# A newly dealt order for a fused linear-attention and feed-forward kernel: all steps from the 60th on, the gates of its loads, and seven small steps on GpSimd

## The chip, the cores and the metric

The kernel runs on one core of a Trainium2 chip. The core has TensorE (PE, matrix products), VectorE (DVE), ScalarE (ACT), GpSimd (POOL) and SyncE (SP), and 16 DMA engines. Each engine works through a list of its own, in order, and waits at semaphores for the others. Results of TensorE land in PSUM, eight banks of 128 partitions x 512 fp32 numbers; everything else lies in SBUF. The metric is the device time of one execution in microseconds: the median of three runs before the change is 351.93 us (350.92 to 352.03).

## The reference

Inputs are q, k and v of 8 batches x 8 heads x 576 positions x 64 features, a feature matrix `w_phi` (64 x 128) and two feed-forward matrices (512 x 2048 and 2048 x 512).

```python
def phi(x):
    proj = np.einsum('bhsd,df->bhsf', x, w_phi)
    proj = proj - np.max(np.abs(proj), axis=-1, keepdims=True)
    return np.concatenate([np.exp(proj), np.exp(-proj)], axis=-1)
q_p, k_p = (phi(q), phi(k))
kv = np.einsum('bhsf,bhsd->bhfd', k_p, v)
z = np.sum(k_p, axis=2)
num = np.einsum('bhsf,bhfd->bhsd', q_p, kv)
den = np.einsum('bhsf,bhf->bhs', q_p, z)[..., None] + 1e-06
```

The attention output num / den, brought to 4608 tokens x 512, is the x of the feed-forward: `h = np.maximum(x @ w_in, 0.0)`, and the result is `(h * h) @ w_out`, 4608 x 512 in fp32.

## The kernel before

**Tiles.** The eight batches are treated one after the other. A batch has 576 tokens: 512 make a feed-forward chunk of their own (chunks 0 to 7), and the remaining 64 of all batches are collected in `xS` and make chunk 8. PE multiplies in bf16, blocks of 128 x 128 against up to 512 columns.

**Attention of a batch.** k and q are needed with their features on the partitions. In batches 0 and 1 PE transposes them itself (`pe_transposes`), and a copy on VectorE or ScalarE moves the block out of PSUM. From batch 2 on one DMA transpose each, issued on SP (`transposed`, L339), makes `kT` and `qT` out of the loaded `xk` and `xq`. `project` multiplies with `w_phi` (L355); the row maximum is taken on VectorE (k: L410, q: L517) and the two exponentials on ScalarE (k: L416, q: L592). The maximum itself goes into v: `em_ops` makes factors of it on ScalarE, `v_ops` multiplies v with them (L443). `kv_ops` sums k features times v on PE (L473, L478) and copies the sum to SBUF (the "kv copy", L196 on VectorE, L198 on ScalarE). `out_ops` multiplies q's features with it (L607), scales by the factor `en` (ScalarE L551, VectorE L619), divides (L627, L631) and turns the result into `xT`: in batch 0 on PE with a copy (L656), later by a DMA transpose on SP (L665).

**Feed-forward of a chunk.** `ffn_in` (L751; for chunk 0 `ffn_in_small`, L762, in pieces of 128 tokens) makes 512 columns of h in a PSUM bank. `relu_sq` takes the relu on ScalarE (L726) or VectorE (L728) into one of four buffers `hr`, and squares it into `h2` (L735). `ffn_out` (L816) sums four times four products to one 128 x 512 output tile, which is copied out of PSUM and stored from SP (L835). For the last tokens stands `last_out` (L780). The feed-forward of chunk c - 1 and c runs on PE beside the attention of later batches, so that PE always has something to do.

**Loads.** All loads of k, q, v, w_in and w_out are issued on GpSimd; they cast fp32 to bf16 on the way. From batch 2 on k, q and v of a batch come in four pieces of two heads each and two short ones for the last 64 tokens. Batches of the same parity share their buffers `xk`, `xq`, `xv`.

**What sets the order.** The program first lists all steps (1731 of them, numbered as they are listed; a step is the group of instructions that one `add` gives). `Plan.arrange` then emits them in the order of the table `ORDER`, with these tables beside it, all written out as numbers:

- `STATES` has a digit for each step that was given to `plan.either`: 1 puts it on the second engine named there. Relus, output copies, kv copies and the copies of transposed blocks can be on ScalarE or VectorE; v products and squares of the first batches or chunks can be on VectorE or GpSimd.
- `BASES` has the PSUM bank of each step that opens one.
- `GATES` names, for loads from batch 2 on, a step that must have ended before the load is issued. As GpSimd works in order, a load also waits for the gates of those ahead of it.
- `FILL` puts warm-up matmuls on PE ahead of a step (L885): the step's number, then bank, count, column.

So the position in `ORDER` counts only against steps of the same engine, and between engines only the data, the buffers and the gates hold a step back.

Of the kernel before, what the change touches and what calls it, by code (L numbers as in the profile page):

```python
# [111 lines left out]
def kernel(  # L112
# [15 lines left out]
    P = 128  # L128
# [47 lines left out]
    LENT = 2  # L176
# [9 lines left out]
    h2 = [ring(f"h2{c}_", 4, [4, TCH]) for c in range(2)]  # L186
# [130 lines left out]
    def attention(b):  # L317
        s2 = b % 2
        pe_in = b < 2
        first = b == 0  # L320
# [125 lines left out]
        def v_ops(g0, g1):  # L446

            gs = [4] if g0 == 4 else list(range(g0, g1))
            for sg in range(2):
# [13 lines left out]
                if b < LENT:  # L463
                    plan.either((o, "POOL", pool_cost(512 * (g1 - g0))))
# [256 lines left out]
    def relu_sq(c, g, dst, toks):  # L721
# [15 lines left out]
        if c < LENT:  # L737
            plan.either((o, "POOL", pool_cost(512)))
# [17 lines left out]
    def ffn_in_small(c, tt, mg):  # L756

        g = Bank(1, "hp")
        def fn():
            for i in range(4):  # L760
                for kc in range(KC):
                    pin(nc.tensor.matmul(out=ps1(g)[:, i * P : (i + 1) * P], lhsT=win[mg][:, kc, i * P : (i + 1) * P],  # L762
                                         rhs=xT[c % NXT][kc // 2][:, tt, kc % 2, :],
                                         start=(kc == 0), stop=(kc == KC - 1)))
        add("PE", pe_cost(16, 0.0565), fn, r=[("win", mg)] + x_toks(c, [tt]),
            w=[g], opens=g, what="f1")
        relu_sq(c, g, h2[c % 2][mg][:, :, tt * P : (tt + 1) * P], [("h2", c % 2, mg * 4 + i, tt) for i in range(4)])
# [266 lines left out]
```

## Time and profile before

| | before |
|---|---|
| median of three runs | 351.93 us |
| profiled execution | 352.42 us |
| its span, first to last instruction | 350.3 us |
| TensorE busy | 337.3 us |
| VectorE busy | 271.6 us |
| ScalarE busy | 228.7 us |
| GpSimd busy | 96.8 us |
| data moved by DMA | 46.69 MB |

The span is that of one execution taken by the profiler; the device time is longer by what lies around it. Matmuls are pipelined, so a busy PE says that one was in flight. In lines of the profile "x<-y" is a step's output and input by the program's names, "xN" a count, and "<- A" behind an idle time tells what ended it. PEld is PE's loading of weights; SPq, ACTq and POOLq are the queues of engines that issue DMAs.

### The profile page before, as it was taken

The numbers are of one execution on the slowest core, as the hardware profiler recorded it, in microseconds if no ns is written. First come the engines' busy times: TensorE is split into PE (matmuls) and PEld (weight loads), VectorE is DVE, ScalarE is ACT, GpSimd is POOL, SyncE is SP. The second block draws the span as 40 slices with busy tenths as digits, with TensorE's granted clock in tenths as the row PEclk, the third lists the DMA queues.
The fourth block names the chain that finished last, engine by engine and source line by source line (L and its number), as shares of the span: only waits on it lengthen the run. The fifth ranks groups of instructions, "written<-read, shape, count | busy, mean of one in ns | idle before, by whom it ended". The sixth has DMA issues, their size and how long they took to land.

```text
span 350.3 us, 8403 instructions
## 1 busy us (share of the span) xinstructions
PE 337.3 (96%) x3335; PEld 191.7 (55%) x3370; DVE 271.6 (78%) x520; ACT 228.7 (65%) x432; POOL 96.8 (28%) x144
## 2 busy tenths in 40 slices
PE   8889999999999999999999989999999999999994
PEld 5669976544654555465546544465455544444451
DVE  4999998899979988898889988789697923745030
ACT  4999897599779775987999684784766111233111
POOL 8735450397518600283100460010000000000000
PEclk9999999999999999999999999999999999999998
DMA  8999989799999997899999999778954521001016
GB/s 100 183 201 202 196 98 144 154 127 156 192 184 134 155 148 150 189 153 117 136 190 164 141 155 165 169 116 144 207 110 77 117 87 67 32 0 60 2 37 173
DMA packets 124327, 46.69 MB, mean 133 GB/s; under 512 B 92800, under 2 KB 119808, under 8 KB 124288
## 3 DMA queue, kind: packets, MB, share of 16 engines
q0 software_dynamic: 45216, 18.36, 46.9%
q1 hardware_dynamic: 78752, 27.50, 39.7%
q8 instruction: 26, 0.43, 0.5%
q10 hardware_dynamic: 320, 0.30, 0.4%
q14 instruction: 13, 0.11, 0.1%
HBM read 36.77 MB, written 9.44 MB: 132 GB/s over the span
## 4 chain that ended last, share of the span: by engine, by line
PE 84%; ACT 5%; DVE 4%; DMA 3%; issue 2%; DVEq 0%; ACTq 0%; POOLq 0%
PE psum L816 32%; PE psum L751 30%; PE psum L607 5%; PE psum L355 5%; PE psum L473 4%; PE psum L762 3%; DMA xT<-xo 2%; DVE va L443 2%; ACT qf L592 2%; PE psum L577 2%; PE psum L780 1%; DMA xk<-in_k_dram 1%; PE psum L478 1%; ACT kp L398 1%; DVE mq L517 1%
## 5 line engine op out<-in xcount | busy, mean ns | idle before, releaser
L816 PE MATMUL psum<-wout,h 128*128 128x512 bf16 x525 | 129.4, 379 | 2.6 <-issue 1.1
L751 PE MATMUL psum<-xT,win 128*128 128x512 bf16 x448 | 107.6, 379 | 1.2 <-DMA xT<-xo 1.2
L726 ACT ACTIVATE hr<-psum 128x512 bf16<-128x512 f32 x99 | 57.1, 596 | 63.4 <-PE psum L751 48.0
L816 PEld LDWEIGHTS <-h 128*128 128x128 bf16 x560 | 51.3, 98 | 55.9 <-issue 0.8
L751 PEld LDWEIGHTS <-win 128*128 128x128 bf16 x512 | 46.9, 98 | 53.6 <-issue 1.9
L735 DVE TENSOR_TENSOR h<-hr 128x512 bf16<-128x512 bf16 x143 | 56.3, 417 | 14.8 <-ACT hr L726 14.2
L592 ACT ACTIVATE qf<-psum 128x1024 bf16<-128x1024 f32 (+1 forms) x50 | 45.8, 945 | 7.6 <-PE psum L577 7.3
L517 DVE TENSOR_REDUCE mq<-psum 128x8 f32<-128x1024 f32 (+1 forms) x40 | 44.1, 1108 | 2.3 <-PE psum L355 1.1
L728 DVE TENSOR_SCALAR hr<-psum 128x512 bf16<-128x512 f32 x45 | 30.5, 686 | 18.8 <-PE psum L751 17.9
L410 DVE TENSOR_REDUCE mk<-psum 128x8 f32<-128x1024 f32 (+1 forms) x35 | 38.1, 1112 | 5.5 <-PE psum L355 4.7
L416 ACT ACTIVATE kp<-psum 128x1024 bf16<-128x1024 f32 (+1 forms) x35 | 32.7, 937 | 14.1 <-DVE mk L410 14.0
L607 PEld LDWEIGHTS <-qf 128*128 128x128 bf16 x640 | 28.2, 97 | 13.1 <-issue 0.9
L619 DVE TENSOR_TENSOR psum<-psum,en 128x520 f32<-128x520 f32 (+1 forms) x40 | 27.7, 699 | 8.7 <-PE psum L607 6.7
L416 ACT ACTIVATE kn<-psum 128x1024 bf16<-128x1024 f32 (+1 forms) x35 | 32.7, 937 | 0.0
L607 PE MATMUL psum<-kv,qf 128*128 128x65 bf16 x640 | 31.2, 193 | 0.1
L443 DVE TENSOR_TENSOR va<-xv,va 64x256 bf16<-64x256 bf16 (+2 forms) x68 | 30.2, 459 | 0.8
L254 POOL DMA_DIRECT2D xv<-in_v_dram x26 | 19.2, 751 | 34.0 <-ACT va L435 8.9
L631 DVE TENSOR_TENSOR xo<-psum,rden 128x512 bf16<-128x512 f32 (+1 forms) x40 | 27.3, 684 | 0.7
L274 POOL DMA_DIRECT2D xq<-in_q_dram x24 | 17.2, 720 | 35.7 <-ACT va L435 13.9
L254 POOL DMA_DIRECT2D xk<-in_k_dram x28 | 20.5, 736 | 12.4 <-ACT va L429 5.2
L473 PE MATMUL psum<-va,kp 128*128 128x65 bf16 x256 | 19.5, 193 | 0.8 <-DVE va L443 0.4
L473 PE MATMUL psum<-va,kn 128*128 128x65 bf16 x256 | 19.5, 193 | 0.0
(68 smaller groups left out, 368.4 us busy)
## 6 DMA issues: line engine op xcount, KB each, us to landing
out_dram<-ot SPq DMA_DIRECT2D x32, 256.0 KB, 2.8
xk<-in_k_dram POOLq DMA_DIRECT2D x26, 128.0 KB, 4.6
xq<-in_q_dram POOLq DMA_DIRECT2D x24, 128.0 KB, 5.8
xv<-in_v_dram POOLq DMA_DIRECT2D x24, 128.0 KB, 5.0
win<-in_moe_w_in_dram POOLq DMA_DIRECT2D x4, 512.0 KB, 11.7
wout<-in_moe_w_out_dram POOLq DMA_DIRECT2D x4, 512.0 KB, 11.7
xq<-in_q_dram POOLq DMA_DIRECT2D x4, 256.0 KB, 6.3
xv<-in_v_dram POOLq DMA_DIRECT2D x2, 512.0 KB, 9.3
```

Source lines behind the costliest of these rows:

```text
L254: pin(nc.gpsimd.dma_start(out=x[:, a * 512 : z * 512].rearrange("p (h x) -> p h x", x=4 * D), in_=src[b][2 * a : 2 * z, 0:512, :].rearrang ...
L410: pin(nc.vector.tensor_reduce(out=mk_view(g), in_=ps2(pj)[:, :, : n * Fd].rearrange("p e (i f) -> p e i f", f=Fd), axis=AX.X, op=ALU.max, ...
L416: pin(nc.scalar.activation(out=dst[slot][:, :, :n, :].rearrange("p e i f -> p e (i f)"), in_=ps2(pj)[:, :, : n * Fd], func=ACT.Exp, scale= ...
L443: pin(engine().tensor_tensor(out=t[:, :, :D].rearrange("p m (x c) -> p m x c", c=2), in0=x.rearrange("p (m x c) -> p m x c", m=n, c=2), in ...
L473: pin(nc.tensor.matmul(out=o[:, sg, hi, :], lhsT=(kp, kn)[sg][kgroup[pr]][:, j % 2, 2 * hi + j // 2, :], rhs=va[s2][sg][:, 8 * pr + 4 * hi ...
L517: pin(nc.vector.tensor_reduce(out=mqb[:, c, :, :n], in_=ps2(pj)[:, :, : n * Fd].rearrange("p e (i f) -> p e i f", f=Fd), axis=AX.X, op=ALU ...
L592: pin(nc.scalar.activation(out=o, in_=i_, func=ACT.Exp, scale=sgn))
L607: pin(nc.tensor.matmul(out=o[:, u // 4, u % 4 * D1 : (u % 4 + 1) * D1], lhsT=(qp, qn)[sg][slot][:, u * m : u * m + P], rhs=kv_sb[s2][:, h ...
L726: pin(nc.scalar.activation(out=hr[sl], in_=ps1(g), func=ACT.Relu))
L735: pin(engine().tensor_tensor(out=dst, in0=i_, in1=i_, op=ALU.mult))
L751: pin(nc.tensor.matmul(out=o, lhsT=win[mc // 4][:, kc, mc % 4 * P : (mc % 4 + 1) * P], rhs=x, start=(kc == 0), stop=(kc == KC - 1)))
L816: pin(nc.tensor.matmul(out=ps1(g), lhsT=h2[c % 2][mc // 4][:, mc % 4, tt * P : (tt + 1) * P], rhs=wout[mc // 4][:, mc % 4, :], start=(mc = ...
```

## The change

The list of the 1731 steps and what each computes stay as they are. The first 60 entries of `ORDER` stay too; all others are in a new order, with new tables `BASES`, `STATES`, `GATES` and `FILL`. The constant `LENT` goes: before, v products of batches 0 and 1 and squares of chunks 0 and 1 could be put on GpSimd; now v products of batch 0, and squares of chunk 0's first two tiles of tokens.

118 steps are on another engine than before. Steps 98, 103 and 104 (v products of batch 0) and 327, 330, 336 and 345 (squares of chunk 0) go from VectorE to GpSimd, and step 515 (a square of chunk 1) goes from GpSimd to VectorE. The others are exchanges between ScalarE and VectorE, after which VectorE has 48 relus (before 45), 12 output copies (14), 16 kv copies (15) and two copies of transposed blocks more; ScalarE has the rest.

On GpSimd the three products stand behind the load of `win` 0 (step 22) and ahead of all that follows: then come steps 24, 23, 34, 25, 28, 35, 27, 30, 32, 33 and 38, and the four squares among 31, 36, 37 and 39. Before, loads of batch 2 stood among these (steps 381, 374, 376, 378, 379, 375, 377, 370); now they all come behind step 39, in the order 377, 374, 380, 381, 375, 379, 372, 376, 370, 378, 371, 373, and behind them 574, 386, 384, 387, 383, 572, 382, 571. On SP the first step is still 389, the transpose of q of batch 2; behind it stand a store (512) and 388, the transpose of k. `FILL` has 64 warm-up matmuls (76 before).

```diff
-    LENT = 2
...
-                if b < LENT:
+                if first:
                     plan.either((o, "POOL", pool_cost(512 * (g1 - g0))))
...
-    def relu_sq(c, g, dst, toks):
+    def relu_sq(c, g, dst, toks, lent=False):
...
         o = add("DVE", dve_cost(256), fn, r=[("hr", sl)], w=toks, what="sq")
-        if c < LENT:
+        if lent:
             plan.either((o, "POOL", pool_cost(512)))
...
-        relu_sq(c, g, h2[c % 2][mg][:, :, tt * P : (tt + 1) * P], [("h2", c % 2, mg * 4 + i, tt) for i in range(4)])
+        relu_sq(c, g, h2[c % 2][mg][:, :, tt * P : (tt + 1) * P], [("h2", c % 2, mg * 4 + i, tt) for i in range(4)], tt < 2)
...
 ORDER = [
...
-    51, 75, 123, 86, 52, 87, 50, 53, 124, 76, 115, 88, 54, 116, 55, 77, 89, 90, 22, 113, 79, 78, 23, 56, 114, 91, 27,
...
-    31, 279, 251, 359, 361, 351, 266, 258, 389, 354, 259, 252, 365, 280, 362, 201, 281, 203, 260, 516, 204, 202, 282,
...
+    51, 75, 123, 86, 52, 49, 113, 76, 77, 87, 114, 115, 53, 50, 124, 22, 79, 88, 78, 103, 54, 55, 80, 90, 117, 74,
+    98, 56, 89, 116, 91, 57, 104, 83, 59, 118, 143, 155, 60, 63, 94, 92, 62, 95, 58, 158, 156, 24, 61, 93, 100, 81,
...
+    310, 372, 376, 524, 300, 311, 291, 301, 292, 528, 370, 556, 273, 302, 529, 293, 378, 389, 274, 512, 440, 313,
...
 GATES = {
-    370: 220, 371: 240, 372: 116, 373: 189, 374: 95, 375: 123, 376: 118, 377: 185, 378: 223, 379: 118, 380: 189,
-    381: 146, 382: 279, 383: 214, 384: 314, 385: 217, 386: 96, 387: 297, 567: 359, 568: 1, 569: 278, 570: 145,
...
-    1173: 1066, 1174: 839, 1175: 944, 1355: 1192, 1356: 1117, 1357: 1117, 1358: 1066, 1359: 1117, 1360: 1078,
-    1361: 1117, 1362: 1214, 1363: 1117, 1364: 1117, 1365: 1117, 1366: 1185, 1367: 1320, 1368: 1394, 1369: 1353,
...
+    370: 263, 371: 238, 372: 171, 373: 239, 374: 157, 375: 168, 376: 245, 377: 234, 378: 179, 379: 357, 380: 181,
+    381: 236, 382: 279, 383: 255, 384: 348, 385: 366, 386: 363, 387: 354, 567: 276, 568: 311, 569: 299, 570: 311,
...
+    1173: 1039, 1174: 1047, 1175: 1074, 1355: 1035, 1356: 992, 1357: 996, 1358: 1020, 1359: 1114, 1360: 1198,
+    1361: 1110, 1362: 1192, 1363: 1078, 1364: 1011, 1365: 1199, 1366: 1188, 1367: 1249, 1368: 1398, 1369: 1208,
...
 FILL = {
-    40: (0, 15, 0), 42: (0, 3, 0), 64: (0, 4, 0), 66: (0, 6, 0), 109: (0, 3, 0), 144: (0, 6, 0), 53: (0, 5, 0),
-    77: (3, 2, 0), 155: (7, 19, 0), 158: (7, 5, 0), 127: (2, 2, 0), 149: (6, 1, 0), 161: (6, 5, 0),
+    40: (0, 15, 0), 42: (0, 3, 0), 64: (0, 4, 0), 66: (0, 6, 0), 109: (0, 3, 0), 144: (0, 6, 0), 113: (0, 5, 0),
+    117: (5, 15, 0), 158: (0, 4, 0), 219: (6, 3, 0),
 }
```

More of the change, by code (lines that the diff above doesn't have):

```diff
@@ L894 @@
     67, 47, 111, 68, 110, 21, 112, 70, 48, 17, 144, 69, 119, 71, 20, 72, 145, 120, 26, 122, 141, 73, 146, 29, 142,
[81 rows of a table removed]
[81 rows of a table added]
 ]
 BASES = (
-    '7762205543351613247724322302602306674447442731320126074760270660422244446264622606176160063720462403'
-    '6376440226246040224115440556605777123504024764140002202442402462567677750767766755002420370621246244'
-    '6422641733061210160110014062624510460664262260150054644505457100420626040500266266201520104005412405'
-    '4450466203010042644646455323343013201315330627045322761544210720376027202404120456561523'
+    '7762105543371243226524376766604764000204002410460662426323446546002620226066066233152721040454002062'
+    '5676022301502602665564774742245043530402260626760024200642226454732655376544704175646420323242446644'
+    '6646100020130030013133122360444222702606002443362376534724357245502040236520020666647722356355447323'
+    '5244204603057024662426473100122260125043044472254073026426711465365440647512527516740126'
 )
 STATES = (
-    '0000000000000000010100110100110100010010000010000010000000000000100000001000100010100111000000001000'
-    '0010000000001010000000100010000101011110000010001000001001001011001000110100000001001100001010001101'
-    '100001100010011100101010011010110011101001101010100000011101001000010000010'
+    '0000001110000000000001100100011100100001011011000011000001000111110000000000111000000011000101001000'
+    '0000100100110011100011000111010010011100100010000110100001101101000101100000000011010010000001000110'
+    '10001101010010001101011111000011010100011000000'
 )
 GATES = {
[11 rows of a table removed]
[11 rows of a table added]
 }
 FILL = {
-    40: (0, 15, 0), 42: (0, 3, 0), 64: (0, 4, 0), 66: (0, 6, 0), 109: (0, 3, 0), 144: (0, 6, 0), 53: (0, 5, 0),
-    77: (3, 2, 0), 155: (7, 19, 0), 158: (7, 5, 0), 127: (2, 2, 0), 149: (6, 1, 0), 161: (6, 5, 0),
+    40: (0, 15, 0), 42: (0, 3, 0), 64: (0, 4, 0), 66: (0, 6, 0), 109: (0, 3, 0), 144: (0, 6, 0), 113: (0, 5, 0),
+    117: (5, 15, 0), 158: (0, 4, 0), 219: (6, 3, 0),
 }
```

171 rows, old and new, of tables (GATES, ORDER) are left out of this document.

## The prediction

> **What bounds the kernel now.** First the page's busy times, then a table of eight stretches, which cuts the span at 12, 20, 29, 60, 72, 200, 210 and 346 us. Its columns are the length, then the busy us of PE, PEld, DVE, ACT and POOL with the number of instructions, PE's clock, DMA share and GB/s.
>
> ```profile
> PE 337.3 (96%) x3335; PEld 191.7 (55%) x3370; DVE 271.6 (78%) x520; ACT 228.7 (65%) x432; POOL 96.8 (28%) x144
> ```
>
> ```profile
> 12.00:20.00 8.00, 7.52 (x89) 5.41 (x89) 7.88 (x20) 7.96 (x24) 5.27 (x8) 1.00 1.55 192
> 20.00:29.00 9.00, 8.22 (x172) 6.94 (x170) 8.93 (x21) 8.45 (x19) 4.25 (x7) 1.00 1.33 201
> 29.00:60.00 31.00, 30.39 (x516) 25.02 (x520) 29.18 (x60) 26.35 (x49) 10.59 (x15) 1.00 1.24 161
> 60.00:72.00 12.00, 11.79 (x131) 6.45 (x132) 10.61 (x19) 6.97 (x15) 4.66 (x8) 1.00 0.88 126
> 72.00:200.00 128.00, 126.67 (x1306) 68.25 (x1318) 115.68 (x209) 106.16 (x196) 50.64 (x75) 1.00 1.11 157
> 200.00:210.00 10.00, 8.77 (x65) 4.05 (x63) 8.71 (x18) 9.10 (x15) 6.56 (x11) 1.00 1.53 160
> 210.00:346.00 136.00, 134.42 (x982) 68.74 (x994) 83.61 (x164) 56.71 (x107) 4.34 (x7) 1.00 0.45 97
> ```
>
> Two regimes are to be seen. From 12 to 29 us VectorE is busy 16.81 of 17 us and ScalarE 16.41: these two set the pace, and PE has holes, some of them filled with the warm-up matmuls of `FILL`. From 29 us on TensorE sets the end: between 29 and 346 us it is idle 317.00 - 312.04 = 4.96 us in all, 1.23 of them between 200 and 210 us. So a gain has two places only: the moment at which the first feed-forward step starts, and those 5 us; what follows the last matmul keeps its steps. A loss has no such limit: whatever PE must wait for past 29 us is added to the end in full, since no later hole of PE is large enough to take it back.
>
> The change keeps the 60 first steps, and it deals out the rest again. The counts of PE's real steps do not change, so what has to be judged is who is late for PE.
>
> **The start (12 to 29 us).** VectorE's own list of this stretch, and the first feed-forward matmuls on PE (`ffn_in_small`, L762); columns are start, length, engine, line, what, count:
>
> ```profile
> 13.05 0.94 DVE L196 COPY kT<-psum 128x256 bf16<-128x256 bf16 x3
> 28.76 0.24 DVE L656 COPY xT<-psum 128x256 bf16<-128x256 bf16 x1
> ```
>
> ```profile
> 29.13 1.06 PE L762 MATMUL psum<-xT,win 128*128 128x128 bf16 x16
> ```
>
> ```profile
> L443 DVE TENSOR_TENSOR va<-xv,va 128x512 bf16<-128x512 bf16 x8 | 3.1, 413 | 0.0
> L619 DVE TENSOR_TENSOR psum<-psum,en 128x520 f32<-128x520 f32 x32 | 22.2, 700 | 4.9 <-PE psum L607 3.0 <-ACT kn L416 1.1 <-ACT hr L726 0.5
> L517 DVE TENSOR_REDUCE mq<-psum 128x4 f32<-128x512 f32 x8 | 5.5, 686 | 0.5 <-PE psum L355 0.2
> L196 DVE COPY qT<-psum 128x512 bf16<-128x512 bf16 x5 | 2.0, 416 | 0.0
> ```
>
> The first feed-forward step needs the two copies of `xT` that end with the row at 28.76. I count what stands in VectorE's queue between the row at 13.05 and that copy. Gone from there: three v products (3 x 0.413), one scaling of num (0.700), the q maximum of chunk 4 (0.686), 2.63 us together, and a reciprocal, which I leave out. New there: two transposed-block copies of 512 columns (2 x 0.416) and a shorter one of 256, at most 1.25 us. One kv copy is exchanged for another. Net 1.4 us less. Not all of it comes through: num (L607) waits for all four kv copies, and these follow the last v product, which in the new queue ends no earlier, because a q maximum now stands ahead of the products. Between 0 and -1.4 us I take a little over the middle, **-0.8 us**: the first feed-forward step at 28.3 us. The 12 fewer warm-up matmuls fill PE's idle time in both versions and cost nothing.
>
> What GpSimd gets: three v products and four squares; one square, the only one it had, goes back to VectorE.
>
> ```profile
> L735 POOL TENSOR_TENSOR h<-hr 128x512 bf16<-128x512 bf16 x1 | 1.0, 1039 | 1.4 <-DVE hr L728 1.4
> 15.52 0.62 POOL L262 DMA_DIRECT2D xk<-in_k_dram  x1 [1.61 <-DMA xv<-in_v_dram]
> DMA to landing us min/median/max: 10.6/11.7/12.4
> ```
>
> The products can start when v has landed (15.5 us), and at 1.04 us each they end near 18.7 us, before VectorE's own products in that queue. Behind them in GpSimd's queue wait the loads of `win` 2 and 1, then `win` 3. The last row above is that of the four `win` loads: by its median, win 2 issued at 18.7 us lands at 30.4 us, 1 us after its first use (29.4 us). I take 0, because these 11.7 us are time in a full queue (192 to 201 GB/s in the first two stretches), and fewer bytes now stand ahead. Bounds 0 and +1.0. VectorE loses seven instructions of 0.41 us and gains one by this move; behind 29 us that only thins its queue, worth 0 to PE.
>
> **The loads of batch 2 (50 to 72 us).** Here I expect the loss. From batch 2 on, k and q reach PE by a load in GpSimd's queue and then a DMA transpose in SP's queue (L339); `GATES` names the step after which a load is issued. Rows of GpSimd, ScalarE, SP and PE:
>
> ```profile
> 47.17 0.70 POOL L254 DMA_DIRECT2D xk<-in_k_dram  x1 [5.15 <-ACT va L429]
> 49.94 0.73 POOL L254 DMA_DIRECT2D xk<-in_k_dram  x1
> 52.13 0.21 ACT L551 ACTIVATE en<-mq 128x8 f32<-128x8 f32 x1
> 50.56 7.39 SPq L339 DMA_TRANSPOSE qT<-xq  x1
> 58.13 3.65 SPq L339 DMA_TRANSPOSE kT<-xk  x1
> 61.83 2.57 SPq L665 DMA_TRANSPOSE xT<-xo  x2
> 65.91 0.40 PE L355 MATMUL psum<-wphi,qT 64*128 64x128 bf16 x8
> 71.38 0.81 PE L751 MATMUL psum<-xT,win 128*128 128x512 bf16 x3
> ```
>
> Before, q of batch 2 was loaded early, the transpose was issued at 50.56 us, and PE's first use came at 65.91 us. The time to landing of such transposes can be read beside the number of instructions on GpSimd in the same stretch, nearly all of them loads (the last figure in brackets of each table row). The landings are those issued at 50.6, at 80.0 and at 112.3 us, and in one row the two issued at 128.1 and 131.1:
>
> ```profile
> DMA to landing us min/median/max: 11.3/11.3/11.3
> DMA to landing us min/median/max: 8.8/8.8/8.8
> DMA to landing us min/median/max: 11.8/11.8/11.8
> DMA to landing us min/median/max: 4.9/5.6/6.3
> ```
>
> ```profile
> 49.00:61.00 12.00, 11.44 (x183) 7.94 (x185) 10.89 (x24) 9.02 (x18) 2.93 (x5) 1.00 1.40 144
> 80.00:89.00 9.00, 8.92 (x71) 4.37 (x71) 8.91 (x19) 8.59 (x18) 7.19 (x10) 1.00 1.19 178
> 112.00:124.00 12.00, 11.93 (x140) 6.57 (x138) 11.05 (x23) 9.75 (x20) 6.31 (x10) 1.00 1.57 152
> 128.00:138.00 10.00, 9.89 (x89) 5.18 (x90) 8.48 (x16) 4.99 (x9) 0.00 (x0) 1.00 0.89 187
> ```
>
> With no load beside it a transpose lands in 4.9 to 6.3 us; with five to ten beside it, in 8.8 to 11.8 us.
>
> In the new lists the last piece of q (step 378) stands behind a piece of k (370) whose gate is step 263, the `en` of batch 1, chunk 0. That step is now at the 94th place of ScalarE's queue; at the same place before stands the row at 52.13 us. Up to that place the queue now has two exponentials of q and one relu more, and three short copies less (0.2 to 0.4 each, about 1.0):
>
> ```profile
> L592 ACT ACTIVATE qf<-psum 128x1024 bf16<-128x1024 f32 x40 | 40.0, 1032 | 4.1 <-PE psum L577 4.0
> L726 ACT ACTIVATE hr<-psum 128x512 bf16<-128x512 f32 x99 | 57.1, 596 | 63.4 <-PE psum L751 48.0 <-DVE h L735 13.9 <-PE psum L647 1.2
> ```
>
> That is 2.06 + 0.60 - 1.0 = 1.7 us more. ScalarE was idle for 4.65 of 31 us from 29 to 60, so part of it goes into idle time: 52.1 to 53.8 us, I take 53.3. Then 370 is issued, and 378 at 54.1 us.
>
> ```profile
> DMA to landing us min/median/max: 2.9/3.1/3.3
> xq<-in_q_dram POOLq DMA_DIRECT2D x24, 128.0 KB, 5.8
> ```
>
> The first row is the two k pieces issued at 47.2 and 48.5 us into a drained queue, which is the case here too, as GpSimd has stood still at 370's gate; the second is the median of all. So q is in at 57.2 us (bounds 57.0 and 59.9), and SP issues its transpose there, 6.6 us later than before. And behind 378 nothing holds the next nine loads back (371, 373, 574, 386, 384, 387, 383, 572, 382): at 0.7 us each they go out from 54.8 to 61 us, beside the transpose. That is the case of 8.8 to 11.8 us; part of the nine is through by 57.2, so I take 9.7: landing at 66.9 us.
>
> PE's first use moves the other way. Ahead of it stand the same steps less five: two of `ffn_out` (L816, 0.86 us each in the row of the chain below) and three short ones, which I put at 0.5 together. That is 2.2 us; and the start is 0.8 us earlier: 65.9 - 3.0 = 62.9 us.
>
> ```profile
> 57.25 0.86 PE psum L816 x4
> ```
>
> PE waits 66.9 - 62.9 = **4.0 us**. Lower bound: the shortest load and the shortest unloaded landing, 57.0 + 4.9 = 61.9, no wait. Upper: 59.9 + 11.8 = 71.7, or 8.8 us. I stand between, nearer to the loaded rows. The rest of the stage asks for the same: behind the transpose of q (SP held for 7.39 us then) come a store, that of k (3.65) and four of `xT` (1.3 each), so `xT` is complete about 57.2 + 7.4 + 0.6 + 3.7 + 5.1 + 2 = 76 us, and the first step of chunk 1 (L751, 71.38 before, 70.8 now, 74.8 after the wait) wants it then. The two waits overlap and are counted once; the 1.2 us between them stay in the range.
>
> **The rest.** Later pieces of k and q are gated on steps of PE's own stream, and move with it. Their leads are shorter than they were, the gates of batch 7 are spread over the stage instead of standing on one step (1117); I put the sum at 0, between -1.2 us (the hole at 208.6 us goes) and +3 us (another transpose lands as late as the one above).
>
> ```profile
> 208.58 0.61 PE L751 MATMUL psum<-xT,win 128*128 128x512 bf16 x2 [1.18 <-DMA xT<-xo]
> ```
>
> **The sum.** The profiled execution took 352.42 us (span 350.3 and 2.1 around it), 0.5 above the median of 351.93. 352.42 - 0.8 + 4.0 = 355.6; against the median 355.1, and I say **355.0 us**.
>
> **Rivals.** *The transposes are in time* (faster). The start's 0.8 us stay, and with the loads of batch 7 spread the hole at 208.6 goes as well: 351.93 - 0.8 - 1.2 = 349.9; without the second 351.1. It decides if q's transpose lands by 62.9 us, thus in 5.7 us or less. For it: the unloaded landings (4.9 to 6.3). Against it: nine loads. 0.22 and 0.06.
>
> *GpSimd stops VectorE* (slower by another way). Seven GpSimd instructions that read SBUF now run where VectorE has its own v products and squares. If each stops VectorE for its whole 1.04 us, 7.3 us are added to a queue that has 31.00 - 29.18 = 1.8 us to spare from 29 to 60 us: 351.93 - 0.8 + 5.5 = 356.6; it decides from 1.8 us on. For it: VectorE is as full there as PE. Against it: products and squares that GpSimd takes no longer stand on VectorE, so few pairs meet. 0.07. [...]
>
> *A later hand-over fails too*: k of batch 3, whose transpose must land by 95 us less the shift, or q of batch 5, adds up to 3 us: 358. 0.10. *Nothing moves*, the gain of the start and a wait of 1 us cancel: 352. 0.07.
>
> **How the numbers follow.** The forecast has 0.48. 0.3% is about what a measurement of this kernel can tell from no change. Faster (below 350.9): 0.22 of the first rival and 0.02 of a forecast with a kind rest, 0.24. Within 0.3%: 0.06 and 0.07, 0.13. Slower: 0.46 + 0.07 + 0.10 = 0.63. The range takes in the first rival and the third: 349.8 to 359.0; the likeliest case alone spans 352.5 (a wait of 1.5 us) to 359.
>
> **What would show it.** PE's first L762 near 28.3 us. In SP's list, L339 of `qT` issued near 57 us, landing in 9 to 12 us. In the waits, PE or PEld L355 idle for about 4 us at 63 to 67 us, released by DMA qT<-xq. Wrong if that transpose lands before 63 us; if VectorE's L443 or L735 are longer than 0.41 us beside POOL; if a new wait of PE past 72 us is larger than 1.5 us.

## The result and the profile after

The changed kernel takes 364.95 us (median of four runs, 363.61 to 365.58) against 351.98 us (350.92 to 352.27) of the kernel before on the same chip: a ratio of 1.0369, 95% interval 1.0333 to 1.0405. It is 13 us slower; the forecast was 3.1 us slower, and its range ended at 359.0. The profiled execution took 365.07 us, span 363.0, so 12.65 us more than the one before (352.42).

Lines of the changed kernel's code stand one lower than before (L815 for L816, L750 for L751). First the page of the changed kernel: busy times, and PE's clock in forty slices.

```profile
PE 342.4 (94%) x3324; PEld 193.4 (53%) x3358; DVE 270.3 (74%) x518; ACT 227.8 (63%) x428; POOL 102.8 (28%) x150
PEclk9999999899999899999999999989999999999999
```

PE is *busy* for 5.1 us more than before (342.4 against 337.3) with the same real work and twelve warm-up matmuls fewer. That, and the three slices in which the clock is below 9, is the first thing to see: some matmuls ran slower. The stretches of the same trace, in the columns that the prediction explained:

```profile
60.00:72.00 12.00, 8.03 (x79) 4.42 (x78) 6.21 (x12) 1.97 (x5) 0.58 (x1) 0.86 1.32 178
110.00:130.00 20.00, 17.21 (x149) 8.69 (x148) 14.70 (x27) 12.99 (x25) 8.82 (x13) 0.91 0.87 136
200.00:210.00 10.00, 9.89 (x102) 5.47 (x102) 8.31 (x16) 6.14 (x15) 3.86 (x6) 1.00 0.92 124
230.00:250.00 20.00, 17.81 (x190) 9.96 (x193) 12.03 (x23) 11.16 (x22) 0.00 (x0) 0.91 0.77 122
```

and two of them in the kernel before:

```profile
110.00:130.00 20.00, 19.87 (x211) 10.72 (x212) 18.38 (x36) 15.71 (x29) 8.93 (x14) 1.00 1.31 145
230.00:250.00 20.00, 19.63 (x224) 11.53 (x226) 16.25 (x31) 11.73 (x22) 2.77 (x4) 1.00 0.81 140
```

Three stretches lose, in two ways. PE stands idle for 12.00 - 8.03 = 3.97, 2.79 and 2.19 us (before 0.21, 0.13 and 0.37); and the clock's mean there is 0.86, 0.91 and 0.91. What ended the idle time, from the waits, the changed kernel's PE first and then the engines that PE waited for:

```profile
PE psum L354 <- DMA qT<-xq: 3.9, 1, 3.9
PE psum L576 <- DVE ot L195: 2.7, 1, 2.7
DVE ot L195 <- DMA out_dram<-ot: 3.3, 1, 3.3
ACT xk L535 <- DMA qf<-xk: 7.2, 2, 4.7
```

**At 68.2 us** PE waits for the transpose of q of batch 2, the wait that was forecast. SP's queue, the time to landing of that transpose, and PE:

```profile
57.33 4.89 SPq L338 DMA_TRANSPOSE qT<-xq  x1
DMA to landing us min/median/max: 10.9/10.9/10.9
68.23 0.61 PE L354 MATMUL psum<-wphi,qT 64*128 64x128 bf16 x8 [3.92 <-DMA qT<-xq]
```

**At 123.0 us** VectorE stood for 3.26 us in front of an output copy whose buffer `ot` was still being stored, and PE needed the PSUM bank that this copy frees. The changed kernel's SP (the row at 115.04 has the stores 727, 709 and, later, 763), the landing of store 709, VectorE, PE:

```profile
113.78 1.17 SPq L664 DMA_TRANSPOSE xS<-xo  x1
115.04 8.27 SPq L834 DMA_DIRECT2D out_dram<-ot  x3
DMA to landing us min/median/max: 6.6/6.6/6.6
122.26 0.69 DVE L195 COPY ot<-psum 128x512 f32<-128x512 f32 x1 [3.26 <-DMA out_dram<-ot]
123.00 0.61 PE L576 MATMUL psum<-qT,wphi 64*128 64x512 bf16 x2 [2.74 <-DVE ot L195]
```

In SP's queue of the kernel before, the store that this copy waits for (709) stands ahead of the transpose to `xS` (494); 727 stood behind that transpose there too:

```profile
102.17 0.53 SPq L835 DMA_DIRECT2D out_dram<-ot  x1
...
109.59 2.47 SPq L665 DMA_TRANSPOSE xS<-xo  x1
```

**At 238.1 us** ScalarE stood for 4.75 us: from batch 5 on the exponentials of q go to a scratch area in `xk` or `xq` and from there through a DMA transpose (L543) to `qf`, and that of chunk 2 had to wait until the transpose of chunk 0 had read the area. PE waited for ScalarE's work behind it, in two pieces of 0.83 and 1.11 us (1.94 together). SP, the landing, ScalarE, PE:

```profile
222.78 5.17 SPq L543 DMA_TRANSPOSE qf<-xk  x1
DMA to landing us min/median/max: 12.1/12.1/12.1
235.02 1.02 ACT L535 ACTIVATE xk<-psum 128x1024 bf16<-128x1024 f32 x1 [4.75 <-DMA qf<-xk]
236.59 0.38 PE L354 MATMUL psum<-wphi,qT 64*128 64x128 bf16 x7 [0.83 <-ACT hr L725]
238.08 0.40 PE L354 MATMUL psum<-wphi,kT 64*128 64x128 bf16 x8 [1.11 <-ACT xk L535]
```

**Behind each of the three** the clock is at half for some 3.4 us: a mean of 0.57 over 4 us, or of 0.72 over 6 us, is 3.4 us at 0.50 and the rest at 1.00. The last row, a part of the second stretch, shows the 0.50, and that a busy share does not tell it: 2.00 of 2.00 us busy.

```profile
68.00:72.00 4.00, 3.77 (x36) 2.24 (x36) 1.61 (x2) 1.38 (x4) 0.00 (x0) 0.57 0.83 183
122.00:128.00 6.00, 5.00 (x54) 2.76 (x53) 5.57 (x11) 2.90 (x5) 2.10 (x4) 0.72 0.68 144
238.00:244.00 6.00, 5.83 (x56) 3.08 (x56) 3.72 (x5) 2.94 (x8) 0.00 (x0) 0.72 0.70 125
124.00:126.00 2.00, 2.00 (x7) 0.71 (x6) 2.00 (x4) 1.59 (x2) 0.10 (x1) 0.50 0.96 221
```

Time lost to it: 4 x 0.43 + 6 x 0.28 + 6 x 0.28 = 5.1 us, a little too much since some of it was idle. The account of the profiled executions: idle in the three stretches (before, from 60 to 72 us and from 200 to 210 us, by the prediction's table) (3.97 - 0.21) + (2.79 - 0.13) + (2.19 - 0.37) = +8.2; clock +5.1; the hole of 200 to 210 us goes, 0.11 instead of 1.23 us idle, -1.1; the first feed-forward step at 28.64 instead of 29.13 us, -0.5. Sum +11.7, of 12.65 measured.

### The profile page after: what moved, and what is told of

Its sections match the earlier page's. It is cut to its first block, busy times and chain, and to the rows that moved or that the text cites. A ratio compares the mean times of both kernels' runs of the same rounds, so it can differ in the third digit from the quotient of the medians.

```text
span 363.0 us, 8407 instructions
## 1 busy us (share of the span) xinstructions
PE 342.4 (94%) x3324; PEld 193.4 (53%) x3358; DVE 270.3 (74%) x518; ACT 227.8 (63%) x428; POOL 102.8 (28%) x150
## 4 chain that ended last, share of the span: by engine, by line
PE 74%; DMA 10%; ACT 7%; DVE 6%; issue 2%; POOL 0%; SPq 0%; DVEq 0%; ACTq 0%; POOLq 0%
PE psum L815 27%; PE psum L750 27%; PE psum L606 5%; PE psum L472 4%; PE psum L354 4%; DMA qf<-xk 3%; DMA qT<-xq 3%; PE psum L761 2%; DVE va L442 2%; DVE mq L516 2%; DMA out_dram<-ot 2%; DMA xq<-in_q_dram 2%; PE psum L576 1%; ACT kp L415 1%; ACT kn L415 1%
## 5 line engine op out<-in xcount | busy, mean ns | idle before, releaser
L815 PE MATMUL psum<-wout,h 128*128 128x512 bf16 x526 | 131.3, 381 | 1.9 <-issue 0.2
L750 PE MATMUL psum<-xT,win 128*128 128x512 bf16 x448 | 111.2, 387 | 0.5 <-DVE mq L516 0.4
L725 ACT ACTIVATE hr<-psum 128x512 bf16<-128x512 f32 x96 | 55.6, 601 | 50.9 <-PE psum L750 33.6
L815 PEld LDWEIGHTS <-h 128*128 128x128 bf16 x560 | 51.4, 98 | 55.9 <-issue 1.2
L750 PEld LDWEIGHTS <-win 128*128 128x128 bf16 x512 | 48.2, 99 | 55.0 <-issue 5.3
L727 DVE TENSOR_SCALAR hr<-psum 128x512 bf16<-128x512 f32 x48 | 32.7, 684 | 21.6 <-PE psum L750 20.3
L618 DVE TENSOR_TENSOR psum<-psum,en 128x520 f32<-128x520 f32 (+1 forms) x40 | 27.7, 701 | 11.3 <-PE psum L606 7.0
L197 ACT ACTIVATE ot<-psum 128x512 f32<-128x512 f32 x23 | 13.7, 595 | 30.5 <-PE psum L815 30.5
L442 DVE TENSOR_TENSOR va<-xv,va 128x1024 bf16<-128x1024 bf16 (+2 forms) x65 | 29.3, 464 | 0.7 <-ACT va L428 0.2
L535 ACT ACTIVATE xk<-psum 128x1024 bf16<-128x1024 f32 (+1 forms) x18 | 15.5, 882 | 12.4 <-DMA qf<-xk 7.2
```

Of the source, the lines that this page charges most:

```text
L442: pin(engine().tensor_tensor(out=t[:, :, :D].rearrange("p m (x c) -> p m x c", c=2), in0=x.rearrange("p (m x c) -> p m x c", m=n, c=2), in ...
L725: pin(nc.scalar.activation(out=hr[sl], in_=ps1(g), func=ACT.Relu))
L750: pin(nc.tensor.matmul(out=o, lhsT=win[mc // 4][:, kc, mc % 4 * P : (mc % 4 + 1) * P], rhs=x, start=(kc == 0), stop=(kc == KC - 1)))
L815: pin(nc.tensor.matmul(out=ps1(g), lhsT=h2[c % 2][mc // 4][:, mc % 4, tt * P : (tt + 1) * P], rhs=wout[mc // 4][:, mc % 4, :], start=(mc = ...
```

## The experiments

The theory at this point: three separate late hand-overs, each followed by a slow stretch. The main rival: the new order runs with too little lead everywhere, and each wait that is removed uncovers another. Each run is the changed kernel with the edit named; ratios are to the kernel before in the same session, and the changed kernel's own is 1.0369. The kernel before stood at 351.98 us beside the changed kernel and at 352.15, 351.58 and 352.08 in the sessions of the runs, so a difference in microseconds to 364.95 can be off by some 0.4. Whole times also move by 1 to 5 us from execution to execution of one kernel. The profiles, one for each kernel, differ in the length of the *other* two waits and in whether the clock falls behind them, so each edit is read in its own stage: idle time plus clock loss, (1 - clock) x length, over 20 us. For the changed kernel that is 4.02 + 1.8 = 5.8 us from 60 to 80 us, 2.79 + 1.8 = 4.6 from 110 to 130, and 2.19 + 1.8 = 4.0 from 230 to 250:

```profile
60.00:80.00 20.00, 15.98 (x144) 8.24 (x145) 13.28 (x22) 8.58 (x18) 0.84 (x2) 0.91 0.91 137
```

### One gate of batch 2 eased

```diff
-    370: 263, 371: 238, 372: 171,
+    370: 171, 371: 238, 372: 171,
```

> The changed kernel with one gate eased: the load of the first piece of k of batch 2 (step 370) waits for step 171 instead of 263, so step 378 behind it in GpSimd's queue goes out some 1.3 to 2 us earlier. Theory (the hand-over of q of batch 2 is late by both its issue and its landing): the transpose of q is issued near 55.8 us instead of 57.3 and still takes some 10.8 us to land, PE's wait of 4.09 us at 68.2 us falls to about 2.5, and the time to about 363.4 us from 364.95. Rival (the gate is the whole cause): the wait is gone and the time is 359 to 360. Second rival (what is won there is given back at the next wait): 364.5 to 365.5.

Measured: 359.39 us, ratio 1.0216 (1.0183 to 1.0250). The landing of the transpose, issued at 55.67 us, the stage, and PE:

```profile
DMA to landing us min/median/max: 9.2/9.2/9.2
60.00:80.00 20.00, 17.07 (x163) 8.42 (x160) 15.58 (x25) 12.54 (x26) 4.08 (x6) 1.00 0.96 146
64.93 0.40 PE L354 MATMUL psum<-wphi,qT 64*128 64x128 bf16 x8 [1.49 <-DMA qT<-xq]
...
74.52 1.24 PE L750 MATMUL psum<-xT,win 128*128 128x512 bf16 x5 [1.44 <-DMA xT<-xo]
```

The time is that of the rival (gate alone), but not for its reason: 1.49 us of the wait stay, and a second one of 1.44 us for `xT` comes out, which the first had covered. The stage loses 2.93 us instead of 5.8, and 1.8 of the 2.9 us gained are the clock, which stays at 1.00. The rest of the 5.6 us came elsewhere: in this execution the clock did not fall from 230 to 250 us either (mean 1.00).

### The loads behind held back

```diff
 GATES = {
+    574: 293,
```

> The changed kernel with one gate added: the seven loads from step 574 on, which stand behind q of batch 2 in GpSimd's queue and go out from 55.9 us beside its transpose, wait for step 293 (ends near 63.9 us). The transpose is issued at 57.3 us as before. Theory (the loads beside it make it slow): it lands in 5 to 7 us instead of 10.85, at 62 to 64 us, PE's wait of 4.09 us at 68.2 is gone or under 0.5, and with the lower clock that follows the wait (1.5 us of further stretch in the stage) the time falls by 4.1 to 5.6 us, to 359.4 to 360.9. Rival (the transpose takes its 10 to 11 us whatever is beside it, since in the kernel before it took 11.34): the wait stays at 3.5 to 4.1 and the time at 364.5 to 365.5.

Measured: 361.28 us (358.55 to 363.61), ratio 1.0268 (1.0201 to 1.0335). The transpose, issued at 56.51 us with two loads still in flight instead of nine, and PE:

```profile
DMA to landing us min/median/max: 6.7/6.7/6.7
73.76 1.46 PE L750 MATMUL psum<-xT,win 128*128 128x512 bf16 x6 [1.87 <-DMA xT<-xo]
```

So the loads beside it do make it slow, 10.9 to 6.7 us, and the wait of 68 us is gone; the stage loses 1.87 us instead of 5.8. (The profiled execution is the fastest of the four, 358.55 us; the median lies just above the expected 359.4 to 360.9.) The loads now stand beside the `xT` transposes, and PE waits there. Both causes of the prediction's term, a late issue and loads beside, are real; neither edit alone clears the stage.

### Four output buffers

```diff
-    ot = ring("ot", 3, [DM], F32)
+    ot = ring("ot", 4, [DM], F32)
...
-            sl = oslot[0] % 3
+            sl = oslot[0] % 4
```

> The changed kernel with four output buffers ot instead of three, so that step 762 (the output copy of chunk 1, tt 3, on VectorE) no longer waits for the store of tt 0, which lands at 122.2 us. Theory (VectorE's idle 3.3 us in front of that copy are the cause of PE's wait of 2.81 us at 123.0): the wait is gone, the clock stays at 1.00 between 120 and 130 us instead of 0.83, and the time falls by 2.8 to 4.0 us, to 361.0 to 362.1. Rival (the wait only moves to the next late item, such as the exponentials of q of batch 3): PE has another hole of 2 us or more between 118 and 135 us and the time is 364 to 365.5.

Measured: 358.97 us, ratio 1.0192 (1.0151 to 1.0233), 2 us below the expected range. In this kernel one buffer is filled again ahead of its store (chunk 7, tile 1), so one output tile is not stored with its own values; that touches only the last 20 us. The copy of step 762 follows the instruction ahead of it (a v product that ends at 119.66) at once, and the stage loses 0.08 us instead of 4.6. In the profiled execution the clock did not fall behind the third wait (1.75 us) either (mean 1.00 from 230 to 250 us), which the expectation had not counted. VectorE and the stage:

```profile
118.98 0.68 DVE L442 TENSOR_TENSOR va<-xv,va 128x1024 bf16<-128x1024 bf16 x1
119.58 0.68 DVE L195 COPY ot<-psum 128x512 f32<-128x512 f32 x1
...
110.00:130.00 20.00, 19.92 (x198) 10.56 (x196) 17.86 (x32) 16.22 (x32) 10.13 (x15) 1.00 1.05 154
```

### The two stores ahead in SP's queue

Steps 727 and 709 stand ahead of 494, with three buffers; nothing else is moved. (In the kernel before, 709 alone stood ahead of it.)

```diff
 ORDER (steps of SP alone)
-    485, 467, 494, 727, 709, 763,
+    485, 467, 727, 709, 494, 763,
```

> The changed kernel with two steps moved in SP's queue alone: the stores of chunk 1, tt 1 and tt 0 (steps 727, 709, ready since 107.5 us) ahead of the transpose 494 of xo of batch 2, chunk 4, for which SP waits until 113.8 us; three output buffers as in the changed kernel. Theory (the order in SP's queue makes the second wait): both stores land before 116 us, the output copy 762 does not wait, PE's wait of 2.81 us at 123.0 is gone, and the time falls by 2.8 to 4.2 us, to 360.8 to 362.2. Rival (three buffers are too few whatever the order, or the loads make the stores late): a wait of over 1 us remains between 115 and 130 us, 363 to 365.5.

Measured: 359.36 us, ratio 1.0201 (1.0165 to 1.0237), 1.4 us below the expected range. SP, with the two stores, and the stage:

```profile
107.80 1.00 SPq L834 DMA_DIRECT2D out_dram<-ot  x2
...
110.00:130.00 20.00, 19.86 (x204) 10.70 (x203) 17.93 (x36) 15.04 (x30) 10.68 (x17) 1.00 1.06 133
```

The stores go out 7 us earlier, and the stage loses 0.14 us. Two steps in one queue were worth 4.5 us. The wait at 123 us is a matter of order; a fourth buffer only hides it.

### The loads of q of batch 7 moved back

Steps 1366, 1364, 1361, 1363 and 1362 stand behind step 1258.

```diff
-    1366: 1188,
+    1366: 1258,
```

> The changed kernel with the five loads of q of batch 7 (steps 1366, 1364, 1361, 1363, 1362; issued from 221.0 to 225.2 us) moved behind step 1258, at some 232 us. Theory (they make the transposing of the exponentials of batch 6, chunk 0, slow: 12.14 us to landing, and ScalarE's next exponential writes into what that transpose reads): that transpose lands in 5 to 8 us, before 231 us, PE's wait of 2.33 us at 238.1 is gone, and with the lower clock behind it the time falls by 2.3 to 4.2 us, to 360.7 to 362.7. Rival (the transpose is slow by the store and the transposes ahead of it, not by the loads): it still takes 10 us or more and the wait stays, 364.5 to 365.5. Second rival: the loads are now late for the transpose of q of batch 7, and PE waits near 250 us instead.

Measured: 361.29 us, ratio 1.0268 (1.0215 to 1.0321). The transpose of chunk 0, now with no load in flight beside it, and PE later:

```profile
DMA to landing us min/median/max: 5.2/5.2/5.2
```

```profile
229.00:249.00 20.00, 19.78 (x226) 11.11 (x224) 15.44 (x31) 14.06 (x28) 4.91 (x8) 1.00 0.89 121
249.98 0.40 PE L354 MATMUL psum<-wphi,qT 64*128 64x128 bf16 x8 [1.20 <-DMA qT<-xq]
```

The five loads alone made that transpose land in 12.1 instead of 5.2 us. The wait at 238 us is gone (0.22 us idle from 229 to 249), and the second rival is right as well: q of batch 7 is now late itself, 1.20 us.

### Warm-up matmuls in the three waits

```diff
 FILL = {
+    440: (2, 36, 0), 665: (0, 26, 0), 1379: (7, 14, 0),
```

> The changed kernel with warm-up matmuls ahead of the three waiting steps: 36 at 440, 26 at 665, 14 at 1379 (3.8, 2.7 and 1.5 us of PE), which need nothing of what PE waits for. The waits stay. Theory (the granted clock falls to 0.5 for some 4 us because PE stood idle, at a cost of 1.4 to 1.9 us behind each of the three): the clock is 1.00 behind the first two waits, and the time falls by 2.5 to 4.5 us, to 360.5 to 362.5. Rival (the slow stretch behind a wait is DMA or VectorE catching up, not the clock): 364.5 to 366.

Measured: 359.23 us, ratio 1.0217 (1.0178 to 1.0255): 5.7 us faster (5.3 by the ratios), more than expected. No load, transpose or store was moved: PE's steps still wait in the same three places, only it multiplies zeros meanwhile, for 3.98, 2.92 and 1.66 us (idle before for 3.92, 2.74 and 1.94). The first filling and the three stretches that correspond to those of half clock:

```profile
63.64 3.98 PE L884 MATMUL psum<-warm 128*128 128x248 bf16 x36
...
63.00:72.00 9.00, 8.84 (x95) 6.16 (x94) 4.69 (x8) 3.60 (x10) 0.00 (x0) 1.00 1.10 179
117.00:126.00 9.00, 8.96 (x103) 6.02 (x102) 6.20 (x13) 5.65 (x11) 2.54 (x4) 1.00 0.71 146
231.00:240.00 9.00, 8.89 (x106) 5.70 (x107) 5.46 (x9) 6.31 (x14) 0.00 (x0) 1.00 0.76 149
```

The clock stays at 1.00 in all three. That separates the loss: some 5 of the 13 us (5.1 by the stretches, 5.3 to 5.7 by this run, whose first feed-forward step also came 0.6 us earlier) are not waits but matmuls at half clock behind them.

### All three eased, with and without GpSimd's seven steps

The gate of 370 eased and the loads from 574 on held to step 320; four buffers, with the store 1659 moved ahead so that every tile is stored; the five loads of batch 7 behind step 1248.

```diff
-    370: 263,          1366: 1188,
+    370: 171, 574: 320, 1366: 1248,
```

> The changed kernel with all three late hand-overs eased: the gate of step 370 on 171 and the seven loads from 574 on held back to step 320 (q of batch 2 and the xT transposes behind it then stand alone), four output buffers ot (with the store 1659 moved ahead of the step that fills its buffer again), and the five loads of q of batch 7 behind step 1248. Theory (the loss is three separate waits and the lower clock behind each): bubbles of PE fall from 26.4 us to about 12, as before the change; PE's steps are 1.85 us shorter (fewer fillers, fewer changes of tiling), the time is 350 to 352 us. Rival (the new order is short everywhere, and each wait removed uncovers another): at least two waits over 1 us remain past 60 us, 354 to 358.

> The same with the three v products and four squares back on VectorE, nothing else. Theory (GpSimd's part is worth only the start): VectorE gets 1.24 us more between 15 and 20 us, the first feed-forward step comes 0.3 to 1.0 us later than 28.6, the four squares hide in VectorE's idle time, and the time is 0.3 to 1.0 us above that of the run with them on GpSimd. Rival (GpSimd stops VectorE while it runs): the time is equal or lower without them, and VectorE's instructions that meet them are longer than their median of 0.41 in the run that has them.

Measured with them on GpSimd: 352.77 us, ratio 1.0032 (1.0007 to 1.0058). On VectorE: 355.21 us, ratio 1.0107 (1.0063 to 1.0151). The transpose of q of batch 2 lands in 4.7 us; one wait over 1 us is left, q of batch 7 again:

```profile
DMA to landing us min/median/max: 4.7/4.7/4.7
240.97 0.40 PE L354 MATMUL psum<-wphi,qT 64*128 64x128 bf16 x8 [1.34 <-DMA qT<-xq]
```

So some 12 of the 13 us are these three places and what follows them. The main rival is right in small: single edits did uncover waits of 1.44, 1.87 and 1.20 us. As the account of the 13 us it falls, since one wait over 1 us is left and not two; the time lies between the two expectations, 0.8 us above the theory's. No run shows that PE's steps are 1.85 us shorter, nor that a change of tiling costs time; what the traces show is warm-up matmuls busy for 10.7 us in the changed kernel and 12.1 in the one before. GpSimd's steps are worth 2.4 us, more than expected; the two intervals together leave that uncertain by some 2 us, and the six times without them spread from 353.9 to 358.35. The profiled executions are 2.85 us apart (352.71 and 355.56): 1.9 of it has come about when the feed-forward matmuls of chunk 0 end, and the rest in waits for transposes from 240 to 250 us (1.16 and 0.93 us against 1.34), of which nothing shows that they go back to GpSimd. The feed-forward matmuls of chunk 0 (count, shortest, median and longest in ns, first and last start), with GpSimd's steps and then without, and behind the latter PE's waits without them:

```profile
L761 PE MATMUL psum<-xT,win x256: 216/219/230, 28.4 to 48.3; 128*128 128x128 bf16 x128
```

```profile
L761 PE MATMUL psum<-xT,win x256: 216/219/230, 29.2 to 50.2; 128*128 128x128 bf16 x128
243.01 0.40 PE L354 MATMUL psum<-wphi,qT 64*128 64x128 bf16 x8 [1.16 <-DMA qT<-xq]
247.03 0.42 PE L606 MATMUL psum<-kv,qf 128*128 128x65 bf16 x8 [0.93 <-DMA qf<-xq]
```

### The loads of batch 7 a little earlier

As the last kernel with GpSimd, but the five loads behind step 1239 instead of 1248.

```diff
-    1366: 1248,
+    1366: 1239,
```

> The changed kernel with the three hand-overs eased, as in the run that eased all three, but with the five loads of q of batch 7 behind step 1239 instead of 1248, 2.5 us earlier, so that they stand beside the transpose of chunk 1 of batch 6, which has time, and not of chunk 2. Theory (what is left of the loss is one late landing: the transpose of q of batch 7 was issued at 234.45 us only, behind that of chunk 2, which took 9.3 us): PE's last wait of 1.51 us at 241.0 is gone, no wait over 0.6 us is left past 60 us, and the time is 350.5 to 351.5, level with the kernel before or up to 0.3% faster. Rival (the loads slow chunk 1 instead and ScalarE waits there): a wait over 1 us stays between 225 and 250 us, 352 to 354.

Measured: 350.98 us (350.54 to 352.08, twelve runs), ratio 0.9980 (0.9968 to 0.9992). The transpose of q of batch 7 lands at 237.0 us and PE does not wait for it. The new order with its hand-overs mended is level with the kernel before or 0.2% faster, at the edge of what can be told. The profiled execution, the slowest of the twelve, has one other hole, of 1.83 us at 82.9, behind a q maximum on VectorE; where that comes from was not tried.

## Why the prediction was wrong, point by point

**The start, -0.8 us: right.** The first feed-forward step came at 28.64 us in the profiled execution (-0.5), and between 27.75 and 28.37 in those of the eight other kernels with the same first steps. The gain is GpSimd's: with its steps back on VectorE it comes at 29.16.

**GpSimd's steps, 0 behind the start: too little.** They are worth about 2.4 us in all, of which 0.8 lie at the start. "Behind 29 us that only thins its queue, worth 0 to PE" does not hold in the traces: the feed-forward steps of chunk 0 end 1.9 us earlier (48.3 against 50.2), 1.1 us more than the start explains.

**GpSimd stops VectorE: no loss by it.** The kernel without GpSimd's steps is slower by 2.4 us, so whatever they may cost VectorE is less than what they take off it. As the prediction said, few pairs meet: in the changed kernel one square of VectorE (from 37.21 us, 0.43 long) touches one of GpSimd (36.29 to 37.34), by 0.13 us, too little to tell anything. From 12 to 45 us VectorE's v products, squares and copies of `qT`, each of 512 columns, take 419, 417 and 415 ns on average in the changed kernel, and 418, 415 and 415 ns in the run without GpSimd's steps. That GpSimd stops VectorE was not shown.

**Batch 2, 4.0 us: right, the size by luck in part.** Issue 57.2 forecast, 57.33 measured; landing 66.9 and 68.2; PE ready for it at 62.9 and 64.3; wait 4.0 and 3.92. The landing came 1.3 us and PE 1.4 us later than forecast, and the two errors cancel. The gate of 370 and the loads beside the transpose were both shown to be causes, and the second wait for `xT`, counted as covered, was covered and came out as 1.44 us when the first was shortened.

**"The rest", 0 between -1.2 and +3: the step that failed.** Its lower half came true (the hole at 208.6 is gone, -1.1). But two waits of 2.74 and some 2 us came in, and neither is of the kind that the step looked at. It went through the hand-overs of k and q and their leads, and judged SP's queue at batch 2 only. SP's queue also carries stores and the transposes of the exponentials; the change moved the store 709 behind a transpose that waits for VectorE (and behind 727, which stood there before), and put five loads beside a transpose on whose reading ScalarE waits. Both can be read off the new order as it stands; what they would cost was not worked out. The third rival ("a later hand-over fails too", 358) had the right form with the wrong hand-overs and a third of the price; "a new wait of PE past 72 us larger than 1.5 us", named as the mark of a wrong forecast, came twice.

**No term for the clock: the other failure.** The prediction gave PE's waits at their length. Behind waits of 3.92, 2.74 and about 2 us came 3.4 us at half clock each, a loss of 1.7 us each; the fillers gave 5.3 to 5.7 us back.

With both, 352.42 - 0.5 + 8.2 - 1.1 + 5.1 = 364.1 against 365.07.

## What to carry to other kernels

When an order is dealt out again, follow each in-order queue step by step, the stores in it too: ask of every entry what stands ahead of it that waits for another engine, and what waits for it to land. A wait of TensorE can cost more than its length: here holes of 2.7 us and more, and some of 1.5 to 2.3 us, were followed by slow matmuls that cost some 1.7 us on top. Look at the granted clock behind a hole, not at the busy share, and while the wait can't be removed, fill it with matmuls that need nothing (5.7 us gained here, in three waits). Bulk loads issued beside a DMA transpose that somebody waits for can make that one late: here it landed in 12.1 us with five loads beside it and in 5.2 us without.

## What the runs showed of the hardware

**Transposes beside loads.** The transpose of q of batch 2 landed in 4.7 us (two loads still in flight), 6.7 (two), 9.2 (nine) and 10.9 us (nine); that of chunk 0 of batch 6 in 5.2 us with none and 12.1 with five. SP is held longer as well, 2.77 us in the first case and 4.89 in the last. In the kernel before the first of them took 11.3 us with five loads in flight, so the count alone does not settle it.

**The clock.** Four holes of 2.7 us and more can be read between 60 and 346 us, and half clock followed each of them: 2.74 and 3.92 us in the changed kernel (0.50 from 124 to 126 us, 0.57 on average from 68 to 72), 4.49 us in the run with four buffers and 3.84 us in the one with the five loads moved (0.50 from 68 to 72 us in both). From 1.5 to 2.3 us it went either way, and not by length alone: behind 1.94 us in two pieces it was 0.50 (240 to 242 us in the changed kernel), behind 1.87 us it stayed at 1.00 (60 to 80 us in the run that held the loads back). Two more stretches, of the run that held the loads back (PE idle for 1.22 us between 230 and 232 us) and of the one with the five loads moved (a hole of 2.31 us that ends at 123.0 us):

```profile
230.00:236.00 6.00, 4.71 (x26) 1.95 (x26) 3.29 (x4) 3.91 (x9) 0.00 (x0) 0.73 0.55 106
```

```profile
122.00:128.00 6.00, 4.58 (x69) 2.89 (x69) 5.56 (x11) 3.70 (x7) 2.28 (x4) 1.00 0.68 144
```

In the first it dropped to a mean of 0.73 (0.50 from 234 to 236 us), in the second, behind 2.31 us, it stayed at 1.00. What decides it besides the length of the hole was not shown; no run tried it.
